# Decay attention and two FFNs: the decay mask is read from rows of powers in SBUF, one load per head on two queues, in place of through HBM

## The chip, the core and the metric

One core of a Trainium2 chip runs the whole program. The metric is device time of one execution in microseconds (us), median of three runs. Five engines work side by side and wait for each other by semaphores: PE (matmul; PEld is its weight load), DVE, ACT and POOL (elementwise), and SP, which here only issues DMA transfers. Sixteen DMA engines carry out the transfers that SP or another engine issues.

## The reference

`q`, `k`, `v` have the shape (2, 8, 768, 64), `lam` one decay per head (8 numbers between 0.97 and 0.99). In blocks of 64 the reference computes causal attention with decay and no softmax, `intra[i, j] = (q_i . k_j) * lam^(i-j)` for `i >= j` and 0 otherwise, plus the share of a running state `kv_state` of 64 x 64 per head, which decays by `lam` per position. The result, as a matrix of 1536 tokens x 512, goes through two FFNs: `(h * tanh(softplus(h))) @ w_out` with `h = x @ w_in` and 2048 hidden columns, then `(g * clip(g + 3, 0, 6) / 6) @ w_out2` in the same sizes. All in fp32.

## The kernel before, in words

The tokens are cut into 12 chunks of 128 (`NCH`), six per batch, and into 3 blocks of 512 (`NBLK`). A chunk is one tile `raw` of 128 x 2048 fp32, loaded in two halves of 512 KB: `load_raw(c, 0)` brings keys and queries with features on partitions, `load_raw(c, 1)` keys and values with positions on partitions. Keys and values come from the host in reversed order of position.

For each chunk, `scores` forms key-query products for 8 heads (two tiles `sc` of 128 x 4 x 128, 16 matmuls). `weigh` multiplies them on DVE by the decay mask into `amat`, and on POOL scales the keys by one column of the same mask (`reverse`, line 170) and the queries by the powers (`lampow`, line 172). `attend` forms the new state `u` (line 191) and the output `o` (lines 197 and 205). `settle` carries the state on and splits `o` into a high and a low part, `X`. Chunks 0 to 3 are done ahead of everything else; the rest are laid between the steps of the FFNs by a written table (`att_at`).

`decay_tables` (lines 116 to 147) makes the mask. It loads `lam` into `small`, writes 127 zeros and a one per head into the HBM tile `z` (line 123), forms 128 powers per head by doubling on DVE (line 129, seven multiplies, into `table`, whose first half is `lampow`), writes them into `z` behind the one (line 135), and reads the mask back with two loads (line 141, 256 KB each). Row `j` of a head's mask is the 128 numbers of that head's row of `z` that start at position `j`, so the 128 rows overlap, each shifted by one number. No partition holds the mask before that.

The FFN weights come as 8-byte numbers. `load_w` stages them and `convert` turns them into fp32 high and low parts, with three passes on ACT and three on DVE per unit (lines 245 to 256, then 67 and 70). `gemm1` (line 272) and `gemm2` (line 285) take three matmul passes per product. They make up 2304 of the matmuls.

All transfers are issued by SP in the order of the code in the prologue (`keep_in_program_order` pins an issue behind what was traced before it on its engine): `lam`, the zeros and the one, `raw` of chunk 0 first half, the first weight unit, the powers, `raw` of chunk 0 second half, the two mask loads, `raw` of chunks 1 to 3, the second weight unit. The rest of the order on each engine is made by a planner that simulates the program. It inserts the semaphore waits too, and the transfers share a small set of semaphores in rotation, so that an issue can wait until an earlier transfer with its semaphore has landed. `warm_up` matmuls on zeros (10, then 16) fill PE while the first data come. ACT's first work after its table load is line 245 on the first weight unit.

Of the kernel before, what the change touches and what calls it, by code (L numbers as in the profile page):

```python
# [7 lines left out]
F32 = mybir.dt.float32  # L8
# [6 lines left out]
ACTF = mybir.ActivationFunctionType  # L15
ALU = mybir.AluOpType
PSUM = bass.MemoryType.PSUM
DRAM = bass.MemoryType.DRAM


@with_exitstack
def decay_attention__mish_ffn__hswish_ffn_kernel(
# [8 lines left out]
    nc = tc.nc  # L31
# [10 lines left out]
    tm2_p = ctx.enter_context(tc.tile_pool(name="tm2", bufs=2, side="right"))  # L42
    tm1_p = ctx.enter_context(tc.tile_pool(name="tm1", bufs=1, side="right"))
    stage_p = ctx.enter_context(tc.tile_pool(name="stage", bufs=2, side="right"))
    dram_p = ctx.enter_context(tc.tile_pool(name="dram", bufs=1, space=DRAM))
    ps_h = ctx.enter_context(tc.tile_pool(name="ps_h", bufs=2, space=PSUM))
    ps_y = ctx.enter_context(tc.tile_pool(name="ps_y", bufs=4, space=PSUM))
    ps_a = ctx.enter_context(tc.tile_pool(name="ps_a", bufs=2, space=PSUM))
# [20 lines left out]
    def split_lo(lo, hi, src):  # L69
        nc.vector.tensor_tensor(out=lo, in0=src, in1=f32(hi), op=ALU.subtract)  # L70

    z = dram_p.tile([8, 256], F32, name="z")
    mask = at1.tile([128, 2, 4, 128], F32, name="mask")
    state = [at1.tile([128, 4, 64], F32, name=f"state{i}") for i in range(2)]
    amat = [at1.tile([128, 4, 128], F32, name=f"amat{i}") for i in range(2)]
# [2 lines left out]
    lampow = table[:, 0].rearrange("p (a i) -> p a i", a=4)  # L78
# [14 lines left out]
    def load_raw(c, i):  # L93
        if c >= NCH:
            return
        if i == 0:
            pool = lent_p if c in (2, 3) else raw_p
            raw_t[c] = pool.tile([128, 2048], F32, tag="raw", name="raw")
        s = slice(i * 1024, (i + 1) * 1024)
        ins = nc.sync.dma_start(out=raw_t[c][:, s], in_=att[c, :, s])  # L100
        if pinned[0]:
            tc.keep_in_program_order(ins)
# [13 lines left out]
    def decay_tables():  # L116
        small = tm1_p.tile([128, 344], F32, tag="th", name="small")
        lam4 = small[:, 0:4].unsqueeze(2)
        head = small[0:8, 8:136]
        tc.keep_in_program_order(nc.sync.dma_start(out=small[:, 0:4], in_=lam))  # L120
        nc.vector.memset(head[:, 0:127], 0.0)
        nc.vector.memset(head[:, 127:128], 1.0)
        tc.keep_in_program_order(nc.sync.dma_start(out=z[:, 0:128], in_=head))
        load_raw(0, 0)
        load_w(*plan[0])
        nc.vector.tensor_copy(lampow[:, :, 0:1], lam4)
        m = 1
        while m < 128:
            nc.vector.tensor_tensor(  # L129
                out=lampow[:, :, m:2 * m], in0=lampow[:, :, 0:m],  # L130
                in1=lampow[:, :, m - 1:m].to_broadcast([128, 4, m]), op=ALU.mult,
            )
            m *= 2
        base = z[0:1, 128:129]
        tc.keep_in_program_order(nc.sync.dma_start(
            out=bass.AP(base.tensor, base.offset, [[256, 2], [512, 4], [1, 128]]), in_=lampow[0:128:64],
        ))
        load_raw(0, 1)
        for h2 in range(2):
            base = z[h2:h2 + 1, 0:1]  # L140
            tc.keep_in_program_order(nc.sync.dma_start(
                out=mask[:, h2],
                in_=bass.AP(base.tensor, base.offset, [[1, 128], [512, 4], [1, 128]]),
            ))
        load_raw(1, 0)
        load_raw(1, 1)

# [83 lines left out]
    def load_w(w, t, half, count):  # L231
        shape = [128, count, 512]
        s = stage_p.tile(shape, U64, tag=f"st{count}", name="st")
        ins = nc.sync.dma_start(out=s, in_=w[t:t + count, half].rearrange("t p n -> p t n"))
        if pinned[0]:
            tc.keep_in_program_order(ins)
        stage_t[t, half] = s
# [163 lines left out]
    nc.scalar.preload_act_table_set("mish")  # L401
    warm_up(10)
    decay_tables()
    load_raw(2, 0)
    load_raw(2, 1)
# [140 lines left out]
```

## Time and profile before

| what | value |
|---|---|
| time, median of 3 runs | 590.46 us (588.24 to 592.97) |
| the profiled execution's own time | 589.52 us |
| its span | 587.5 us |
| PE busy | 577.5 us (98%) |
| DVE, ACT, POOL busy | 270.5, 246.8, 14.8 us |
| bytes through the DMA engines | 50.27 MB |
| mean granted TensorE clock | 1.0 |

The span is the profiled stretch of one execution, the time that of the whole execution; the rows below have their zero at the span's start. Busy shares are means over a prologue (chunks 0 to 3, up to 27.8 us), a stretch in which the FFN steps, the other chunks and the conversion of the weights share the engines, and a long rest of FFN steps alone.

### The profile page before, as it was taken

How to read it: one execution, taken by the hardware profiler on the slowest of the kernel's cores; microseconds unless marked ns; L12 is line 12 of the kernel's file. 1: busy time of each engine (PE TensorE's matmuls, PEld its weight loads, DVE VectorE, ACT ScalarE, POOL GpSimd, SP SyncE). 2: the span in 40 equal slices, each digit the busy share in tenths (PEclk: the TensorE clock that was granted, in tenths of full speed). 3: DMA queues.
4: the chain of work that ended last, by engine and by line, in shares of the span. 5: the costliest groups of instructions: out<-in, count | busy, mean ns of one | idle time of the engine just before them, and what ended most of it. 6: DMA issues, size and time to landing. Idle time of an engine off the chain costs nothing.

```text
span 587.5 us, 7414 instructions
## 1 busy us (share of the span) xinstructions
PE 577.5 (98%) x3034; PEld 470.4 (80%) x3034; DVE 270.5 (46%) x400; ACT 246.8 (42%) x408; POOL 14.8 (3%) x20
## 2 busy tenths in 40 slices
PE   7999999999999999999999999999999999999997
PEld 3877788888888888888888888888888888888885
DVE  4799886423666665511667862222222222222221
ACT  2477764215666665512566652212422222421222
POOL 1600100000000000000000000000000000000000
PEclk9999999999999999999999999999999999999999
DMA  7977754201444333200243220000100000100001
GB/s 222 411 281 254 232 179 144 73 1 73 118 134 143 134 117 108 72 1 0 83 140 137 73 71 0 2 0 1 71 1 0 2 0 1 71 1 0 1 0 71
DMA packets 15546, 50.27 MB, mean 86 GB/s; under 512 B 1674, under 2 KB 2714, under 8 KB 15514
## 3 DMA queue, kind: packets, MB, share of 16 engines
q1 hardware_dynamic: 15514, 49.82, 24.8%
q8 instruction: 23, 0.38, 0.3%
q14 instruction: 9, 0.07, 0.0%
HBM read 46.66 MB, written 3.15 MB: 85 GB/s over the span
## 4 chain that ended last, share of the span: by engine, by line
PE 91%; DMA 4%; DVE 2%; ACT 1%; POOL 0%; issue 0%; SPq 0%; ACTq 0%; POOLq 0%
PE y L285 43%; PE h L272 43%; DMA st<-w 2%; PE sc L154 2%; PE o L205 1%; PE o L197 1%; PE u L191 1%; DMA mask<-z 1%; DVE W L70 1%; ACT st L245 0%; DMA z<-table 0%; DVE st L253 0%; ACT st L246 0%; POOL raw L170 0%; DVE table L129 0%
## 5 line engine op out<-in xcount | busy, mean ns | idle before, releaser
L272 PE MATMUL h<-X,W 128*128 128x512 f32 x1152 | 279.4, 391 | 0.0
L272 PEld LDWEIGHTS h<-X,W 128*128 128x128 f32 x1152 | 214.9, 188 | 46.6 <-issue 1.4
L285 PE MATMUL y<-g,W 128*128 128x512 f32 x576 | 138.8, 389 | 0.9 <-ACT W L67 0.8
L285 PE MATMUL y<-W,g 128*128 128x512 f32 x576 | 138.0, 389 | 0.0
L285 PEld LDWEIGHTS y<-g,W 128*128 128x128 f32 x576 | 107.9, 188 | 23.9 <-ACT W L67 0.9
L285 PEld LDWEIGHTS y<-W,g 128*128 128x128 f32 x576 | 108.1, 188 | 22.4
L70 DVE TENSOR_TENSOR g<-x,g 128x512 fp32r<-128x512 f32 x96 | 66.3, 690 | 74.5 <-ACT g L308 44.8
L318 DVE SCALAR_TENSOR_TENSOR x<-x,h 128x512 f32<-128x512 f32 x48 | 33.0, 688 | 141.5 <-ACT x L311 141.3
L311 ACT ACTIVATE x<-h 128x512 f32<-128x512 f32 x48 | 28.8, 599 | 140.8 <-PE h L272 140.5
L253 DVE SCALAR_TENSOR_TENSOR st<-st 128x512 int32<-128x512 int32 (+1 forms) x57 | 43.1, 757 | 38.9 <-ACT st L246 38.8
L245 ACT ACTIVATE st<-st 128x512 f32<-128x512 f32 (+1 forms) x57 | 41.8, 733 | 43.0 <-DMA st<-w 41.4
L67 ACT ACTIVATE W<-st 128x512 fp32r<-128x512 f32 (+1 forms) x57 | 41.4, 728 | 31.7 <-DVE st L256 31.6
L70 DVE TENSOR_TENSOR W<-st,W 128x512 fp32r<-128x512 f32 (+1 forms) x57 | 43.4, 766 | 23.4 <-ACT W L67 22.5
L307 ACT ACTIVATE x<-h 128x512 f32<-128x512 f32 x48 | 28.5, 595 | 57.4 <-PE h L272 57.4
L67 ACT ACTIVATE g<-x 128x512 fp32r<-128x512 f32 x48 | 30.4, 633 | 32.2 <-DVE x L318 32.0
L256 DVE SCALAR_TENSOR_TENSOR st<-st 128x512 int32<-128x512 int32 (+1 forms) x57 | 43.2, 757 | 1.5
L246 ACT ACTIVATE st<-st 128x512 int32<-128x512 uint16 (+1 forms) x57 | 41.2, 723 | 0.0
L308 ACT ACTIVATE g<-h 128x512 fp32r<-128x512 f32 x48 | 28.4, 592 | 0.0
L179 DVE TENSOR_TENSOR amat<-sc,mask 128x512 f32<-128x512 f32 x24 | 16.1, 686 | 8.0 <-PE sc L154 4.5
L67 ACT ACTIVATE X<-o 128x512 fp32r<-128x512 f32 x12 | 7.1, 590 | 24.2 <-PE o L205 18.7
L154 PEld LDWEIGHTS sc<-raw 64*128 64x128 f32 x192 | 12.6, 187 | 5.1 <-issue 2.6
L154 PE MATMUL sc<-raw 64*128 64x128 f32 x192 | 15.1, 285 | 1.1 <-DVE state L220 1.0
(33 smaller groups left out, 138.0 us busy)
## 6 DMA issues: line engine op xcount, KB each, us to landing
st<-w SPq DMA_DIRECT2D x50, 512.0 KB, 3.3
raw<-att SPq DMA_DIRECT2D x24, 512.0 KB, 4.9
st<-w SPq DMA_DIRECT2D x7, 1024.0 KB, 7.2
out<-o SPq DMA_DIRECT2D x12, 256.0 KB, 2.0
mask<-z SPq DMA_DIRECT2D x2, 256.0 KB, 3.9
small<-lam SPq DMA_DIRECT2D x1, 2.0 KB, 1.6
z<-small SPq DMA_DIRECT2D x1, 4.0 KB
z<-table SPq DMA_DIRECT2D x1, 4.0 KB
```

The costliest lines, as they stand in the source:

```text
L67: nc.scalar.activation(out=hi, in_=src, func=ACTF.Copy)
L70: nc.vector.tensor_tensor(out=lo, in0=src, in1=f32(hi), op=ALU.subtract)
L154: nc.tensor.matmul(sc[h2][:, p, :], lhsT=kT[r, p, :], rhs=qT[r, p, :], start=True, stop=True)
L245: nc.scalar.activation(out=hf, in_=hf, func=ACTF.Copy, scale=2.0 ** -112)
L246: nc.scalar.activation(out=lo16[..., 0] if sign_on_act else lo, in_=lo16[..., 1], func=ACTF.Copy, scale=2.0 ** -13, bias=2.0 ** -14 - 0.5,)
L253: nc.vector.scalar_tensor_tensor(out=lo, in0=hi, scalar=-2 ** 31, in1=lo, op0=ALU.bitwise_and, op1=ALU.bitwise_or)
L256: nc.vector.scalar_tensor_tensor(out=hi, in0=hi, scalar=3, in1=lo, op0=ALU.logical_shift_left, op1=ALU.bitwise_or)
L272: nc.tensor.matmul(h, lhsT=W[t][:, a, kt * 128:kt * 128 + 128], rhs=X[k][:, b, kt, :], start=(kt, a, b) == order[0], stop=(kt, a, b) == or ...
L285: nc.tensor.matmul(y[e], lhsT=l, rhs=r, start=(first and i == 0), stop=(last and i == 2),)
L307: nc.scalar.activation(out=x, in_=h, func=ACTF.Mish)
L311: nc.scalar.activation(out=x, in_=h, func=ACTF.Relu, bias=3.0)
L318: nc.vector.scalar_tensor_tensor(out=r, in0=r, scalar=6.0, in1=h_t.pop(n), op0=ALU.min, op1=ALU.mult)
```

## The change

The HBM tile `z` and the three kinds of transfers through it are gone. `z` becomes an SBUF tile of 128 x 4 x 256 in a slot of the weight staging pool (tag `st2`, two slots): on every partition, for each of four heads, 127 zeros, a one and 128 powers. Partitions 0 to 63 hold the powers of the heads with `h2 = 0`, partitions 64 to 127 those with `h2 = 1`, as `lam` is laid out. The zeros and the one are now written by POOL, the powers are formed directly in `z` by the same DVE instructions, and one more DVE copy brings them to `lampow`. The mask is read with eight transfers of 64 KB, each from one partition (`h2 * 64 + p * 16`), as 128 overlapping rows of 512 B, to 128 partitions. Four are issued on SP (`p` = 0, 2), four on ACT (`p` = 1, 3). `load_raw(0, 1)` stands behind them in the code; before, it stood ahead of the mask loads.

```diff
     def decay_tables():
         small = tm1_p.tile([128, 344], F32, tag="th", name="small")
         lam4 = small[:, 0:4].unsqueeze(2)
-        head = small[0:8, 8:136]
+        z = stage_p.tile([128, 4, 512], F32, tag="st2", name="z")[:, :, 0:256]
+        pw = z[:, :, 128:256]
         tc.keep_in_program_order(nc.sync.dma_start(out=small[:, 0:4], in_=lam))
-        nc.vector.memset(head[:, 0:127], 0.0)
-        nc.vector.memset(head[:, 127:128], 1.0)
-        tc.keep_in_program_order(nc.sync.dma_start(out=z[:, 0:128], in_=head))
+        nc.gpsimd.memset(z[:, :, 0:127], 0.0)
+        nc.gpsimd.memset(z[:, :, 127:128], 1.0)
         load_raw(0, 0)
         load_w(*plan[0])
-        nc.vector.tensor_copy(lampow[:, :, 0:1], lam4)
+        nc.vector.tensor_copy(pw[:, :, 0:1], lam4)
         m = 1
         while m < 128:
             nc.vector.tensor_tensor(
-                out=lampow[:, :, m:2 * m], in0=lampow[:, :, 0:m],
-                in1=lampow[:, :, m - 1:m].to_broadcast([128, 4, m]), op=ALU.mult,
+                out=pw[:, :, m:2 * m], in0=pw[:, :, 0:m],
+                in1=pw[:, :, m - 1:m].to_broadcast([128, 4, m]), op=ALU.mult,
             )
             m *= 2
-        base = z[0:1, 128:129]
-        tc.keep_in_program_order(nc.sync.dma_start(
-            out=bass.AP(base.tensor, base.offset, [[256, 2], [512, 4], [1, 128]]), in_=lampow[0:128:64],
-        ))
+        nc.vector.tensor_copy(lampow, pw)
+        for h2 in range(2):
+            for p in range(4):
+                src = z[h2 * 64 + p * 16:h2 * 64 + p * 16 + 1, p, 0:1]
+                queue = nc.sync if p % 2 == 0 else nc.scalar
+                tc.keep_in_program_order(queue.dma_start(
+                    out=mask[:, h2, p], in_=bass.AP(src.tensor, src.offset, [src.ap[0], [1, 128], [1, 128]]),
+                ))
         load_raw(0, 1)
-        for h2 in range(2):
-            base = z[h2:h2 + 1, 0:1]
-            tc.keep_in_program_order(nc.sync.dma_start(
-                out=mask[:, h2],
-                in_=bass.AP(base.tensor, base.offset, [[1, 128], [512, 4], [1, 128]]),
-            ))
         load_raw(1, 0)
         load_raw(1, 1)
```

## Rows read from the trace of the kernel before

**Rows 1.** Windows: us, busy (count) of PE, PEld, DVE, ACT, POOL; clock, DMA share, GB/s.

```profile
0.00:12.00 12.00, 9.16 (x44) 4.05 (x44) 5.07 (x16) 3.17 (x4) 0.30 (x5) 1.00 0.66 194
12.00:28.00 16.00, 14.49 (x241) 12.10 (x240) 9.91 (x18) 4.68 (x8) 10.78 (x12) 1.00 1.01 401
28.00:60.00 32.00, 31.06 (x231) 24.03 (x232) 30.16 (x38) 24.29 (x33) 0.00 (x0) 1.00 0.78 272
100.00:300.00 200.00, 200.00 (x997) 164.59 (x997) 98.80 (x149) 97.37 (x174) 0.62 (x1) 1.00 0.26 85
```

**Rows 2.** Chain that ended last, prologue: start us, us, what.

```profile
4.47 2.52 DMA z<-table
...
7.50 4.24 DMA mask<-z
...
15.49 1.07 POOL raw L170
```

**Rows 3.** Timeline of SP's issues: start us, us, line, tiles, count.

```profile
0.74 0.38 SPq L120 DMA_DIRECT2D small<-lam  x1
...
1.69 0.36 SPq L100 DMA_DIRECT2D raw<-att  x1
2.09 0.43 SPq L234 DMA_DIRECT2D st<-w  x1
...
5.12 0.40 SPq L100 DMA_DIRECT2D raw<-att  x1
7.07 0.94 SPq L141 DMA_DIRECT2D mask<-z  x2
8.05 3.68 SPq L100 DMA_DIRECT2D raw<-att  x6
```

**Rows 4.** Windows of 1 us: the mask loads, then whole rows of `raw`.

```profile
9.00:10.00 1.00, 1.00 (x6) 0.29 (x4) 0.69 (x1) 0.25 (x1) 0.00 (x0) 1.00 1.00 257
...
16.00:17.00 1.00, 0.40 (x13) 0.40 (x14) 1.00 (x3) 0.54 (x1) 1.00 (x2) 1.00 1.04 426
```

**Rows 5.** Timeline of ACT and DVE up to the second chunk.

```profile
2.39 0.17 DVE L126 COPY table<-small 128x4 f32<-128x4 f32 x1 [1.12 <-DMA small<-lam]
...
7.03 0.66 ACT L245 ACTIVATE st<-st 128x512 f32<-128x512 f32 x1 [5.01 <-DMA st<-w]
8.29 0.69 DVE L253 SCALAR_TENSOR_TENSOR st<-st 128x512 int32<-128x512 int32 x1 [3.85 <-ACT st L246]
...
10.44 0.69 DVE L70 TENSOR_TENSOR W<-st,W 128x512 fp32r<-128x512 f32 x1 [0.73 <-ACT W L67]
11.05 1.47 DVE L179 TENSOR_TENSOR amat<-sc,mask 128x512 f32<-128x512 f32 x2
13.75 0.42 DVE L220 COPY state<-u 128x256 f32<-128x256 f32 x1 [1.23 <-PE u L191]
...
15.75 1.29 DVE L179 TENSOR_TENSOR amat<-sc,mask 128x512 f32<-128x512 f32 x2 [1.57 <-PE o L197]
```

**Rows 6.** Timeline of PE, from the warm-up to the second chunk.

```profile
1.19 4.95 PE L86 MATMUL wp<-wz 128*128 128x512 bf16 x13 [1.19 <-DVE wz L81]
...
7.17 2.98 PE L86 MATMUL wp<-wz 128*128 128x512 bf16 x13
...
11.79 0.43 PE L197 MATMUL o<-amat,raw 128*64 128x128 f32 x2 [1.65 <-DVE amat L179]
...
14.17 0.97 PEld L154 LDWEIGHTS sc<-raw 64*128 64x128 f32 x16 [0.27 <-DMA raw<-att]
...
15.26 0.65 PE L197 MATMUL o<-amat,raw 128*64 128x128 f32 x6
```

**Rows 7.** Timeline of POOL: the table's copy, the second chunk's keys.

```profile
12.90 0.61 POOL L428 COPY table<-mask 128x512 f32<-128x512 f32 x1
...
15.49 1.06 POOL L170 TENSOR_TENSOR raw<-raw,mask 128x512 f32<-128x512 f32 x1 [0.61 <-DMA raw<-att]
```

**Rows 8.** SP's own waits: line, what for, us in total, times, longest.

```profile
SPq L100 <- DMA raw<-att: 6.0, 1, 6.0
```

More of the change, by code (lines that the diff above doesn't have):

```diff
@@ L17 @@
 PSUM = bass.MemoryType.PSUM
-DRAM = bass.MemoryType.DRAM
 @with_exitstack
@@ L44, in decay_attention__mish_ffn__hswish_ffn_kernel @@
     stage_p = ctx.enter_context(tc.tile_pool(name="stage", bufs=2, side="right"))
-    dram_p = ctx.enter_context(tc.tile_pool(name="dram", bufs=1, space=DRAM))
     ps_h = ctx.enter_context(tc.tile_pool(name="ps_h", bufs=2, space=PSUM))
@@ L70, in split_lo @@
         nc.vector.tensor_tensor(out=lo, in0=src, in1=f32(hi), op=ALU.subtract)
-    z = dram_p.tile([8, 256], F32, name="z")
     mask = at1.tile([128, 2, 4, 128], F32, name="mask")
```

## The prediction

> **What bounds the kernel now.** I read the windows by stage first. From 28 us on PE is busy in 31.06 of 32 us, and from 100 to 300 us in all of it [rows 1]: the long rest is matmuls in a fixed number, and nothing in the change touches them. PE can only gain or lose time ahead of that, in the prologue. There, from 0 to 12 us, PE shows 9.16 us busy, but most of it is the two warm-up batches of 4.95 and 2.98 us [rows 6], which are filler. From 12 to 28 us the DMA share is 1.01 at 401 GB/s [rows 1]: the transfers are then at their limit, and in order.
>
> Then I read the chain of waits through the prologue [rows 2]. It runs through the powers' way into HBM (2.52 us from 4.47) and the mask's way back (4.24 us from 7.50). At 15.49 it stands at POOL's scaling of the second chunk's keys, which had idled 0.61 us for its half of `raw` [rows 7]. So two things set the pace: the mask up to 11.74, and behind it the stream of `raw` halves that SP could issue only after the mask loads (5.12, 7.07, 8.05) [rows 3]. Shortly before, PE's scores of chunk 1 wait for `raw` too, and the last six matmuls of chunk 0's output stand behind them in PE's order, done at 15.91 [rows 6]. A shift of that stream by x us shifts the end by nearly x us, since PE is full afterwards.
>
> **The change, part by part.**
>
> *The first transfers.* Without the write of zeros SP issues the first half of `raw` right behind `lam`, at 0.74 + 0.38 = 1.12 in place of 1.69 [rows 3], 0.57 us earlier; the first weight unit likewise. ACT started on that unit at 7.03 [rows 5]; now about 6.5.
>
> *POOL's memsets and DVE's new copy.* 128 x 508 and 128 x 4 zeros and ones on POOL: between nothing and the 0.61 us that its copy of 128 x 512 takes [rows 7]. I take 0.6. POOL has 0.30 us of work up to 12 us [rows 1], and DVE waits for `lam` until 2.39 [rows 5], so this is hidden; without that cover it is 0.6 us. The two small DVE memsets go from the same gap: no gain. The copy into `lampow` lies between 0.42 (128 x 256 copy) and 0.69 us (a 128 x 512 pass with two inputs) [rows 5]; it sits in DVE's idle 3.85 us before 8.29, and the mask loads read `z`, not `lampow`. Cost nothing; uncovered, up to 0.7. The seven multiplies keep their shapes and still end near 4.45.
>
> *The removed trip.* The 2.52 us of writing the powers go entirely [rows 2]. Late next is the mask's own transfer.
>
> *The eight issues.* An issue takes 0.36 to 0.61 us of its queue [rows 3], so four take 1.4 to 2.4 us on each, from 4.47 on. ACT idles 5.01 us before 7.03 [rows 5], and its line 245 now stands behind its four issues: about 6.5, no cost so long as these wait for nothing else. On SP the second half of chunk 0 moves from 5.12 to at least 6.1, and the next six halves from 8.05 to about 6.5 or later. An issue can also wait for an earlier transfer's landing, as one did for 6.0 us [rows 8]; here those are the mask loads and the first unit, behind which the `raw` halves stand anyway. Extra cost zero, included in the next item.
>
> *The transfer itself* is the large unknown: the trace before has no load that reads all its rows out of one partition. The bound below is the mask load before, 512 B pieces from a few KB of HBM, when all sixteen engines together moved 257 GB/s [rows 4]: 524,288 B take 2.0 us. The bound above comes from asking what one partition can give. No row shows one source partition feeding more than one engine's worth of data. An engine moves 426/16 = 26.6 GB/s on long rows and 257/16 = 16.1 GB/s on 512 B pieces [rows 4]. At these rates a 64 KB load takes 2.46 or 4.1 us, and the four that stand one behind another in a queue 9.8 or 16.3 us. I take 9.8: the limit is then one of the memory's side, which the length of a piece does not cut, and the two queues draw from different partitions side by side.
>
> [...]
>
> *The sum.* The mask loads on SP start behind the first unit, at 6.5, and end at 16.3. Behind them on the same queue come three `raw` halves, each 524,288 B at 401 GB/s [rows 1] = 1.3 us: the last lands at 20.2, where 15.49 was the time before [rows 2]. From there the order of work is the one of before, 4.7 us later: 589.52 + 4.7 = **594.2 us**. The base is the profiled execution, 0.94 us under the median shown; I leave it uncorrected. No change, in the sense of 1%, which is about what a measurement of this kernel can tell (5.9 us: below 584.6 or above 596.4).
>
> **Rivals.**
>
> *A. The partition is no bottleneck: 586.8 us, chance 0.33.* The eight loads move like the old ones, 2.0 us behind 6.5, and `raw` lands at 9.8, 11.1 and 12.4, over 3 us earlier. Then DVE is late next: its passes on the first unit end 0.57 us earlier than 11.13, at 10.6, its two mask products (0.69 each) end at 12.0, chunk 0's output about 1.0 later, and the product of chunk 1 starts at 13.0 in place of 15.75 [rows 5]: 2.7 us gained. For it: the old loads read a region as small and were not slow. Against: that was HBM, not one partition.
>
> *B. One partition gives only what an engine draws in 512 B pieces: 600.7 us, slower, chance 0.15.* 16.3 us for the masks; the third half at 6.5 + 16.3 + 3.9 = 26.7, 11.2 us late. Its place is the source partition. It decides "slower" once the shift is over 6.9 us, that is masks over 12.0 us, or a partition under 21.8 GB/s. For it: each row starts 4 B further on, so the pieces are as ragged as the old ones. PE would also idle longer. The granted clock is 1.00 in every window of rows 1, yet the first batch of 13 warm-ups, after 1.19 us of idleness, took 4.95 us and the second 2.98 [rows 6], so a few matmuls after a long wait may be slower; I price this at zero, since the waits for `raw` hide it.
>
> *C. The two queues give no overlap: 604 us, chance 0.07.* The change would then not do what it says. If an engine that stands at one partition's data holds up the other queue's, the eight loads go in series: 8 x 2.46 = 19.7 us, the third half at 30.1, 14.6 late. For it: both queues feed the same sixteen engines, whose share is what the windows count. Against: sixteen engines needn't stand at the same partition together. [...]
>
> **How the numbers follow.** Forecast 0.45, A 0.33, B 0.15, C 0.07. The forecast's own range is 589.5 (four partitions serving at once, 4.9 us in place of 9.8) to 597. All together: 586 to 600 leaves out C, half of B and the lower edge of A, about 0.2. Slower by over 1%: B, C and a tenth of the forecast's case, 0.27. Faster: the edge of A, 0.03. Within 1%: 0.70.
>
> **What would show it.** In the changed kernel: the zeros' and the powers' transfers gone, the first halves issued 0.57 us earlier; the eight issues within about 2 us of 4.47 on SP and ACT; the median time to landing of mask loads growing along each queue by about 2.5 us per load (forecast), 0.5 or less (A), 4 (B), 5 (C); a DMA share near 1 at about 53 GB/s between 7 and 16 us; `raw` of chunk 1 landing near 20 (forecast) or 12 (A); POOL's second scaling there; PE idle up to 18; and from 28 us on the same stages as before, shifted. The prediction is wrong if landings stay close together, if other work of PE fills the wait, or if the planner lays the prologue out in another order.

## The result, and the profile after

The changed kernel took 598.55 us in the median of four runs (596.04 to 605.77) beside 589.9 for the kernel before; the ratio is 1.0108 [1.0074, 1.0143]. (The ratio leaves out disturbed runs on either side, so it is not the quotient of the medians.) So it is slower by some 6.4 us, just past the prediction's 1% bound, which the interval still holds. It lies inside the 586 to 600 that the prediction gives to all its cases together, but above the 589.5 to 597 of the forecast's own case, and 4.3 us above its number. The profiled execution took 598.51 us, span 596.5, which is 9.0 us more than the profiled one before. That one had a mean granted clock of 1.00, and executions of one kernel differ in it: of fifty of the kernel before that were timed beside the experiments, the four at 1.00 took 588.1 to 589.2 us, the three at 0.988 595.2 to 596.6. So the 9.0 are laid against a good execution.

Windows of the changed kernel by stage (columns as in [rows 1]):

```profile
0.00:12.00 12.00, 9.59 (x42) 4.22 (x42) 2.52 (x10) 2.23 (x3) 0.77 (x6) 1.00 0.65 119
12.00:28.00 16.00, 8.81 (x74) 7.10 (x76) 5.71 (x9) 1.51 (x3) 5.29 (x6) 0.57 0.87 273
28.00:60.00 32.00, 31.80 (x334) 25.81 (x333) 29.12 (x40) 22.80 (x32) 6.74 (x7) 1.00 0.83 297
...
100.00:300.00 200.00, 200.00 (x1038) 164.53 (x1034) 97.39 (x147) 96.82 (x173) 1.24 (x2) 1.00 0.27 86
```

Against [rows 1] the loss is all in the prologue. From 12 to 28 us PE ran 74 matmuls instead of 241. The granted clock was 0.57 there, and 1.00 before. From 100 to 300 us PE is busy throughout at a clock of 1.00, as before.

Timeline of SP in the changed kernel (answers to [rows 3]), then of ACT and of POOL (answer to [rows 5, 7]):

```profile
1.20 0.41 SPq L97 DMA_DIRECT2D raw<-att  x1
...
4.55 5.57 SPq L136 DMA_DIRECT2D mask<-z  x4
10.17 8.34 SPq L97 DMA_DIRECT2D raw<-att  x7
```

```profile
4.55 6.45 ACTq L136 DMA_DIRECT2D mask<-z  x4
11.05 0.65 ACT L240 ACTIVATE st<-st 128x512 f32<-128x512 f32 x1 [9.04 <-issue]
```

```profile
16.70 0.61 POOL L423 COPY table<-mask 128x512 f32<-128x512 f32 x1 [15.41 <-DMA mask<-z]
17.64 1.33 POOL L165 TENSOR_TENSOR raw<-raw,mask 128x512 f32<-128x512 f32 x1 [0.33 <-DMA raw<-att]
21.72 1.06 POOL L165 TENSOR_TENSOR raw<-raw,mask 128x512 f32<-128x512 f32 x1 [2.75 <-DMA raw<-att]
```

The last mask load is there at 16.70 (11.74 before, [rows 2]), the second half of chunk 0 at 17.64, that of chunk 1 at 21.72 (15.49 before). Each queue takes 5.6 to 6.5 us for its four issues, and ACT's first conversion stands behind them until 11.05.

PE of the changed kernel, from the end of the warm-up to the first `gemm1` (answers to [rows 6]):

```profile
8.66 2.32 PE L83 MATMUL wp<-wz 128*128 128x512 bf16 x10
17.71 1.98 PE L192 MATMUL o<-amat,raw 128*64 128x128 f32 x16 [6.73 <-DMA raw<-att]
20.39 2.08 PE L149 MATMUL sc<-raw 64*128 64x128 f32 x16 [0.70 <-DMA raw<-att]
23.25 1.29 PE L192 MATMUL o<-amat,raw 128*64 128x128 f32 x6 [0.78 <-DVE amat L174]
24.47 2.07 PE L149 MATMUL sc<-raw 64*128 64x128 f32 x14
26.47 1.02 PE L186 MATMUL u<-raw 128*64 128x64 f32 x16
27.42 0.49 PE L149 MATMUL sc<-raw 64*128 64x128 f32 x2
27.84 0.69 PE L186 MATMUL u<-raw 128*64 128x64 f32 x16
...
38.18 3.01 PE L267 MATMUL h<-X,W 128*128 128x512 f32 x12
```

Two things are to be seen. The order is not that of [rows 6]: `o` of chunk 0 comes first, and its `u`, second before, only at 26.47. And a group of 16 score matmuls takes 2.08 us where it took 1.16 before. The clock in windows of 1 us says why (last three columns: clock, DMA share, GB/s):

```profile
12.00:13.00 1.00, 0.00 (x0) 0.00 (x0) 0.00 (x0) 0.24 (x1) 0.00 (x0) 1.00 0.68 36
13.00:14.00 1.00, 0.00 (x0) 0.00 (x0) 0.67 (x2) 0.00 (x0) 0.00 (x0) 0.80 0.74 86
14.00:15.00 1.00, 0.00 (x0) 0.00 (x0) 0.62 (x2) 0.00 (x0) 0.00 (x0) 0.50 1.10 294
...
26.00:27.00 1.00, 1.00 (x14) 0.78 (x14) 0.00 (x0) 0.00 (x0) 0.00 (x0) 0.50 0.61 250
27.00:28.00 1.00, 1.00 (x18) 0.81 (x16) 0.42 (x1) 0.00 (x0) 0.01 (x1) 0.88 0.28 102
```

PE had nothing to do from 10.98 to 17.71. Within that wait the clock fell to half, 0.50 of full speed, and came back only behind 27 us; 0.80 and 0.88 as means of their windows put the two changes at about 13.6 and 27.2.

The first `gemm1` thus starts 10.4 us later than before (27.80). From there to the end of the span it is 558.3 us, before 559.7: 1.4 us are regained, and 9.0 stay.

### The profile page after: what moved, and what is told of

Read it like the earlier page. It is cut to its first block, busy times and chain, and to the rows that moved or that the text cites. A ratio compares the mean times of both kernels' runs of the same rounds, so it can differ in the third digit from the quotient of the medians.

```text
span 596.5 us, 7428 instructions
## 1 busy us (share of the span) xinstructions
PE 582.0 (98%) x3034; PEld 474.4 (80%) x3034; DVE 270.7 (45%) x399; ACT 246.0 (41%) x408; POOL 16.5 (3%) x22
## 4 chain that ended last, share of the span: by engine, by line
PE 89%; DVE 4%; DMA 3%; ACT 1%; SPq 1%; POOL 1%; issue 1%; ACTq 0%; DVEq 0%; POOLq 0%
PE h L267 42%; PE y L280 42%; PE sc L149 2%; DMA raw<-att 1%; PE o L192 1%; DVE st L248 1%; PE o L200 1%; SPq L136 1%; DMA st<-w 1%; DVE W L68 1%; DVE st L251 1%; PE u L186 1%; ACT st L241 1%; DVE amat L174 1%; SPq L97 0%
## 5 line engine op out<-in xcount | busy, mean ns | idle before, releaser
L192 PE MATMUL o<-amat,raw 128*64 128x128 f32 x192 | 15.1, 293 | 7.7 <-DMA raw<-att 6.7
L149 PEld LDWEIGHTS sc<-raw 64*128 64x128 f32 x192 | 15.0, 215 | 6.6 <-issue 3.1
L149 PE MATMUL sc<-raw 64*128 64x128 f32 x192 | 17.8, 315 | 1.7 <-DMA raw<-att 0.9
```

The lines of the kernel that those rows point to most:

```text
L149: nc.tensor.matmul(sc[h2][:, p, :], lhsT=kT[r, p, :], rhs=qT[r, p, :], start=True, stop=True)
```

## The experiments

Milestones in us from the span's start. "Masks" is the start of POOL's first operation on a complete mask (line 423), "chunk 0" PE's first matmul that uses the mask. All rows but the first have one and the same order of PE's groups between the last two milestones, so that they can be laid side by side.

| kernel | masks | chunk 0 | first `gemm1` | between |
|---|---|---|---|---|
| before (other order) | 11.74 (last load lands) | 11.79 | 27.80 | 16.01 |
| b1_raw_behind | 11.09 | 13.55 | 30.12 | 16.57 |
| x5_hbm | 11.66 | 14.75 | 33.08 | 18.33 |
| x6_half_rows | 11.57 | 12.93 | 33.56 | 20.63 |
| x2_step4 | 13.14 | 16.43 | 34.62 | 18.19 |
| x8_interleaved | 13.34 | 15.76 | 35.83 | 20.07 |
| changed | 16.70 | 17.71 | 38.18 | 20.47 |
| x4_one_queue | 17.01 | 18.81 | 39.81 | 21.00 |
| x1_one_partition | 25.45 | 26.97 | 49.00 | 22.03 |

The times don't follow from these milestones alone. From the first `gemm1` to the end of the span it is 558 to 560 us in the profiles of the kernel before, the changed one, b1_raw_behind, x2_step4, x4_one_queue and x8_interleaved, but 562.4 in x5_hbm, 565.0 in x6_half_rows, 565.6 in x10_first_raw_ahead and 565.8 in x1_one_partition. In these four the granted clock fell a second time: its mean from 60 to 100 us is 0.91, 0.87, 0.91 and 0.87, and 1.00 in the others. As an example x10_first_raw_ahead, where PE was idle for 2.1 of the 10 us in which it fell:

```profile
60.00:70.00 10.00, 7.86 (x53) 5.76 (x53) 8.17 (x12) 7.82 (x11) 1.47 (x1) 0.94 0.76 226
70.00:80.00 10.00, 10.00 (x68) 7.98 (x69) 6.31 (x8) 6.05 (x7) 0.76 (x1) 0.72 0.41 156
```

So the milestones, and not the times, show what an edit does to the prologue.

### The source: one, two or four groups of partitions

x1_one_partition: the four heads of a half all come from one partition.

```diff
-                src = z[h2 * 64 + p * 16:h2 * 64 + p * 16 + 1, p, 0:1]
+                src = z[h2 * 64:h2 * 64 + 1, p, 0:1]
```

> The eight loads read from partitions 0 (h2 = 0) and 64 (h2 = 1) only, so that both queues draw from one partition at a time; the order on every engine is that of the changed kernel. Theory of the source (one partition, or what it shares with its neighbours, hands out some 25 GB/s however many engines ask): the four loads of a half now share one source, 256 KB at 25 GB/s = 10.5 us per half, the masks end near 26 us in place of 16.7, the time goes to about 608 us. Rival, each piece read from SBUF is slow by itself, or eight issues are: nothing changes, masks at 16.7 us, about 598 us.

Measured: masks at 25.45, where 26 was expected, and 616.54 us (a single run) in place of 608. In its profile the clock is at 0.50 from 16 to 36 us, besides the second fall.

x2_step4: partitions 0, 4, 8, 12 (and 64 more) in place of 0, 16, 32, 48.

```diff
-                src = z[h2 * 64 + p * 16:h2 * 64 + p * 16 + 1, p, 0:1]
+                src = z[h2 * 64 + p * 4:h2 * 64 + p * 4 + 1, p, 0:1]
```

> Source partitions h2*64 + 4p in place of h2*64 + 16p, same order on every engine. If the limit is the single partition, nothing changes: masks at 16.7 us, about 598 us. [...] If loads from neighbours close by share more than those 16 apart, it gets slower.

Measured: masks at 13.14, and not near the 16.7 that a limit of the single partition would leave, but a ratio of 1.0158 [1.0104, 1.0213] and a median of 598.34 us (595.88 to 602.26): masks and first `gemm1` come 3.6 us earlier than in the changed kernel, and the time doesn't show it over the spread of the executions. The same two windows of x1_one_partition, of the changed kernel and of x2_step4, a stretch in which nearly only mask loads run:

```profile
7.00:9.00 2.00, 2.00 (x16) 1.05 (x15) 0.00 (x0) 0.00 (x0) 0.00 (x0) 1.00 0.66 25
9.00:11.00 2.00, 2.00 (x10) 0.77 (x8) 0.00 (x0) 0.00 (x0) 0.00 (x0) 1.00 0.65 25
```

```profile
7.00:9.00 2.00, 2.00 (x16) 1.03 (x15) 0.00 (x0) 0.00 (x0) 0.00 (x0) 1.00 0.71 51
9.00:11.00 2.00, 1.98 (x10) 0.69 (x7) 0.00 (x0) 0.00 (x0) 0.00 (x0) 1.00 0.73 73
```

```profile
7.00:9.00 2.00, 2.00 (x16) 1.05 (x15) 0.00 (x0) 0.00 (x0) 0.00 (x0) 1.00 0.70 103
9.00:11.00 2.00, 2.00 (x10) 0.73 (x8) 0.13 (x1) 1.23 (x2) 0.00 (x0) 1.00 0.71 89
```

From 7 to 9 us these are 25, 51 and 103 GB/s (from 9 us on, loads of the second half, with sources of their own, probably run into those of the first). One partition gives 25 GB/s. In the changed kernel the four partitions of a half (0, 16, 32, 48) give only twice that, in x2_step4 (0, 4, 8, 12) four times. So the former make up two sources, and the latter four. Partitions 0 and 16 are probably not the ones that share: the first loads on SP and ACT, which read them, land 4.8 and 5.0 us after their issue in the changed kernel, nearly as soon as the quickest load of x1_one_partition (4.6), while their 131,072 B at 25 GB/s from one source would move for 5.2 us, an estimate. Which partitions do share, no run shows. The DMA share of 0.66, 0.71 and 0.70 at 25, 51 and 103 GB/s says how little that column tells here. It also shows that the limit is not that one engine carries a source, since 0.66 of sixteen engines is more than ten.

x4_one_queue: all eight loads on SP.

```diff
-                queue = nc.sync if p % 2 == 0 else nc.scalar
+                queue = nc.sync
```

> All eight mask loads on SP. Theory of the source: one source at a time, 8 x 2.5 = 20 us from 6.5, masks near 26 us, about 608 us. Rival, the two queues give no overlap: unchanged, 16.7 us, 598 us.

Measured: 600.91 us (a single run), masks at 17.01 instead of 16.70, against 26 expected. A miss: loads that stand in one queue are carried out side by side, and one queue draws as fast as two. Its eight issues took 7.52 us together, each load landed 4.4 to 6.5 us after its issue, and from 7 to 9 us 50 GB/s moved, beside 51 in the changed kernel:

```profile
7.00:9.00 2.00, 2.00 (x12) 0.94 (x11) 0.64 (x1) 1.22 (x2) 0.00 (x0) 1.00 0.70 50
9.00:11.00 2.00, 1.61 (x8) 0.52 (x6) 0.74 (x2) 0.67 (x1) 0.00 (x0) 1.00 0.69 59
```

x6_half_rows: only the second half of each mask row is loaded, 256 B in place of 512, and POOL writes zeros into the first 64 columns; those of the mask are left out.

```diff
-        nc.vector.tensor_copy(lampow, pw)
+        nc.vector.tensor_copy(lampow, pw); nc.gpsimd.memset(mask[:, :, :, 0:64], 0.0)
...
-                src = z[h2 * 64 + p * 16:h2 * 64 + p * 16 + 1, p, 0:1]
+                src = z[h2 * 64 + p * 16:h2 * 64 + p * 16 + 1, p, 64:65]
...
-                    out=mask[:, h2, p], in_=bass.AP(src.tensor, src.offset, [src.ap[0], [1, 128], [1, 128]]),
+                    out=mask[:, h2, p, 64:128], in_=bass.AP(src.tensor, src.offset, [src.ap[0], [1, 128], [1, 64]]),
```

> Each of the eight loads brings only the second half of every row (256 B in place of 512 B, 128 pieces each); the first 64 columns of the mask are set to zero, so part of the decay product is left out. If the source gives so many bytes a second, the masks need half the time and end near 11.5 us in place of 16.7. If it gives so many pieces a second, they still end near 16.7.

Measured: masks at 11.57, 59 GB/s from 7 to 9 us; 600.34 us (a single run). Half the bytes in as many pieces take 7.0 us from the first issue at 4.56, where the changed kernel takes 12.15. So the limit is one of bytes, not of pieces, which takes away rival B's rate of 16.1 GB/s. As an estimate from the two: 262,144 B less save 5.14 us, so the whole 524,288 B take 10.3 us and begin to move at 6.4.

### Without the slow source

x5_hbm: the powers' rows go once to HBM, and the eight loads read from there, on both queues as in the changed kernel.

```diff
-        nc.vector.tensor_copy(lampow, pw)
+        nc.vector.tensor_copy(lampow, pw); zd = dram_p.tile([8, 256], F32, name="zd"); base = zd[0:1, 0:1]; tc.keep_in_program_order(nc.sync.dma_start(out=bass.AP(base.tensor, base.offset, [[256, 2], [512, 4], [1, 256]]), in_=z[0:128:64]))
...
-                src = z[h2 * 64 + p * 16:h2 * 64 + p * 16 + 1, p, 0:1]
+                src = zd[2 * p + h2:2 * p + h2 + 1, 0:1]
...
-                    out=mask[:, h2, p], in_=bass.AP(src.tensor, src.offset, [src.ap[0], [1, 128], [1, 128]]),
+                    out=mask[:, h2, p], in_=bass.AP(src.tensor, src.offset, [[1, 128], [1, 128]]),
```

> The changed kernel with its eight loads on two queues and raw behind them, but the rows (zeros, one, powers) are written once to HBM from two partitions and read from there. Theory of the source: pieces from HBM take 27 ns and not some 230, the eight loads end by about 11 us, and the time is near the kernel before, 589 to 592 us. Rival, the structure of the change is at fault (eight issues, two queues, raw behind the mask, the planner's new order): the time stays at 596 to 599 us.

Measured: masks at 11.66, as in the kernel before, and yet a ratio of 1.0098 [1.0062, 1.0134]. The slow source is not the whole loss. Chunk 0 starts at 14.75, since its second `raw` half stands behind the mask loads on SP, and the clock falls here too, for a shorter time, to a mean of 0.80 from 13 to 16 us and 0.72 from 16 to 20: PE's first two groups take 1.97 and 1.89 us. The first `gemm1` is 5.1 us earlier than in the changed kernel, but 4.1 of them are lost again behind it in the profiled execution, with the second fall of the clock; so the time, which can't be told from the changed kernel's 1.0108, is no measure of what the source costs.

b1_raw_behind: the kernel before, with nothing but `load_raw(0, 1)` moved to its place in the changed one.

```diff
-        load_raw(0, 1)
         for h2 in range(2):
...
             ))
+        load_raw(0, 1)
         load_raw(1, 0)
```

> The kernel before, mask through HBM and all on SP, with one line moved: the second half of raw of chunk 0 is issued behind the two mask loads, as in the changed kernel. The planner answers with the changed kernel's order on PE (chunk 0's output first, its state update u only after most of the scores of chunk 2). Theory that part of the loss is this move and the order it brings, whatever the source of the mask: the masks land as before (11.7 us), that half of raw at 12.5 to 14.5 us, chunk 0 starts there, and the first gemm1 runs at 30.5 to 33 us in place of 27.80, the time is 592 to 595 us (3 to 5 us slower). Rival, the move costs only the landing (0.7 us) and the rest of the loss needs the SBUF source or the eight issues: first gemm1 near 28.5 us, 590 to 591 us.

Measured: 1.0043 [1.0014, 1.0072], 2.5 us where 3 to 5 were expected. PE of b1_raw_behind:

```profile
13.55 1.09 PE L197 MATMUL o<-amat,raw 128*64 128x128 f32 x16 [3.46 <-DMA raw<-att]
14.76 1.16 PE L154 MATMUL sc<-raw 64*128 64x128 f32 x16
16.70 0.43 PE L197 MATMUL o<-amat,raw 128*64 128x128 f32 x2 [0.78 <-DVE amat L179]
17.30 0.44 PE L197 MATMUL o<-amat,raw 128*64 128x128 f32 x4 [0.17 <-DVE amat L179]
17.66 1.16 PE L154 MATMUL sc<-raw 64*128 64x128 f32 x14
18.75 0.69 PE L191 MATMUL u<-raw 128*64 128x64 f32 x16
19.36 0.49 PE L154 MATMUL sc<-raw 64*128 64x128 f32 x2
19.78 0.69 PE L191 MATMUL u<-raw 128*64 128x64 f32 x16
...
22.07 1.16 PE L154 MATMUL sc<-raw 64*128 64x128 f32 x16
...
30.12 3.06 PE L272 MATMUL h<-X,W 128*128 128x512 f32 x12
```

Moving that one load is enough for the planner's other order (`o` first, `u` late), at the full clock throughout. It is the ruler for the changed kernel: group for group, the changed kernel stands 4.16 us later at the first `o`, 5.63 at the first scores, 6.55 at the next `o`, 6.81, 7.72, and 8.06 from the second `u` on, up to the first `gemm1`. The shift grows only while the clock is at half, and stops growing when it is back.

### The clock

x3_warm: 46 warm-up matmuls in place of 16 before the scores of chunk 1, so that PE is busy until the masks land.

```diff
-    warm_up(16)
+    warm_up(46)
```

> 46 in place of 16 warm-up matmuls on zeros ahead of the scores of chunk 1, which fill PE's idle time from 10.98 to 17.71 us (30 more at 0.23 us = 6.8 us); the planner also lays chunk 0's state update earlier. Theory that 4 us of the loss come from the granted clock of 0.50 between 14 and 27.6 us: the clock stays at 1.00, the matmuls of 17.7 to 28 us take 4.7 instead of 8.9 us, and the time falls by 2.5 to 4.5 us, to 594 to 596 us. Rival, the prologue is bound by the arrival of raw and PE's pace doesn't matter: no gain (within 1 us of 598).

Measured: 601.08 us, 1.0178 [1.0139, 1.0218]: a miss. PE was busy up to 17.5 and the clock at 1.00 up to 20, but the planner laid the groups in another order (scores of chunk 1 first, at 19.75), with 2.27, 2.36 and 2.28 us of waits in it, and the clock fell twice later (means of 0.64 from 20 to 24 and 0.84 from 32 to 36). It changes two things and decides nothing.

p1_pinned, p2_pinned_warm: to hold the order fixed, every compute instruction from the second warm-up on is pinned to the order of the code, and p2_pinned_warm has 56 warm-ups in place of 16 besides.

```diff
-    nc = tc.nc
+    class Pinned:
...
+            return lambda *a, **k: tc.keep_in_program_order(op(*a, **k)) if held[0] else op(*a, **k)
...
+    nc = Core()
...
-    warm_up(16)
+    held[0] = True
+    warm_up(56)
```

> The changed kernel with every compute instruction from the second warm-up on pinned to the order of the code on its engine, so that p2 can be compared with it. PE then waits from the end of the warm-up (11 us) for raw of chunk 1 (20 us). By itself it only sets the base: the whole program in the order of the code may cost some us or tens of us, 600 to 640 us.

> p1_pinned with 56 in place of 16 warm-up matmuls in the second batch; the order on PE, DVE, ACT and POOL is that of p1 otherwise. Theory, the granted clock of 0.50 after PE's long wait costs time of its own: the clock stays at 1.00 up to the first gemm1, chunk 0 to 2 run at the full pace, and the first gemm1 and the time come 2 to 4 us earlier than in p1. Rival, the slow matmuls hide behind the arrival of raw and behind DVE: less than 1 us.

Measured: 677.34 and 676.24 us (1.1471 [1.1427, 1.1516] and 1.1458 [1.1406, 1.151]), over the 600 to 640 expected of p1_pinned, since the pinned order costs far more than what is studied here; the first `gemm1` at 37.60 and 36.69. From 12 to 20 us and from 20 to 28 us the clock was 0.58 and 0.78 in p1_pinned and 1.00 in p2_pinned_warm, and that gave 0.9 us, where 2 to 4 were expected. The theory as it stood then fell. PE of p2_pinned_warm shows where the rest of it went:

```profile
19.87 1.16 PE L36 MATMUL sc<-raw 64*128 64x128 f32 x16 [0.32 <-DMA raw<-att]
...
23.23 1.16 PE L36 MATMUL sc<-raw 64*128 64x128 f32 x16 [0.71 <-DMA raw<-att]
...
35.60 1.16 PE L36 MATMUL sc<-raw 64*128 64x128 f32 x14 [2.12 <-DVE state L36]
```

In this order the second scores at 23.23 wait for `raw`, and the scores at 35.60 for DVE (2.11 us in p1_pinned as well). The slow groups of p1_pinned fill the first of these waits (24.05 there, without a wait).

In the planner's own order the price is larger, and can be read without a new kernel. x4_one_queue and b1_raw_behind have the same order, the same wait of 0.78 us for DVE, and no wait for `raw` between chunk 0's start and `gemm1`. PE of x4_one_queue:

```profile
18.81 1.98 PE L192 MATMUL o<-amat,raw 128*64 128x128 f32 x16 [8.20 <-DMA raw<-att]
20.71 2.08 PE L149 MATMUL sc<-raw 64*128 64x128 f32 x16
23.57 1.29 PE L192 MATMUL o<-amat,raw 128*64 128x128 f32 x6 [0.78 <-DVE amat L174]
...
28.57 1.12 PE L186 MATMUL u<-raw 128*64 128x64 f32 x16
29.48 1.49 PE L192 MATMUL o<-amat,raw 128*64 128x128 f32 x10
30.90 1.51 PE L200 MATMUL o<-raw,state 64*64 64x128 f32 x16
32.34 1.16 PE L149 MATMUL sc<-raw 64*128 64x128 f32 x16
...
39.81 3.02 PE L267 MATMUL h<-X,W 128*128 128x512 f32 x12
```

The stretch takes 21.00 us here and 16.57 there. Up to the scores at 32.34, which stand at 22.07 in b1_raw_behind, the groups that ran at half the clock cost 5.0 us; 0.6 come back behind them, where b1_raw_behind waits for DVE. That comparison came after the runs, and no edit changes the clock alone in this order. Executions of one kernel do differ in it: of b1_raw_behind's, the three at a mean clock of 1.00 took 590.2 to 591.6 us, the four at 0.988 595.0 to 598.0. So a lower clock goes with a longer time in one and the same program; where it fell in these is not recorded.

### Can the change be saved

x8_interleaved: x2_step4 with the loop over heads outside, so that each queue alternates between the halves, eight sources in all.

```diff
-        for h2 in range(2):
-            for p in range(4):
-                src = z[h2 * 64 + p * 16:h2 * 64 + p * 16 + 1, p, 0:1]
+        for p in range(4):
+            for h2 in range(2):
+                src = z[h2 * 64 + p * 4:h2 * 64 + p * 4 + 1, p, 0:1]
```

> Source partitions h2*64 + 4p as in x2_step4, and the loads alternate between the two halves, so that all eight sources are in use at once; the order on PE, POOL and SP is that of the changed kernel. So far the masks ended at 25.4 us with one source per half, 16.7 with the changed kernel's, 13.1 with four per half. Theory, each such group of sources gives about 25 GB/s and engines that are ahead draw from the next: 8 x 25 = 200 GB/s, 512 KB in 2.6 us, masks near 10 us, raw behind them, first gemm1 at 31 to 32 us, 591 to 594 us. Rival, four sources are already enough and the rest of the wait is the issue of the loads: masks stay near 13 us, 595 us or more.

Measured: 111 GB/s from 7 to 9 us against 103, masks at 13.34, ratio 1.0138 [1.0084, 1.0193]: eight sources in turn give hardly more than four. What holds them back is not shown: 25 GB/s from each of the eight would make 200, an estimate, and the issues on each queue took from 4.54 to 9.05, so that the issuing may be the limit here.

x9_raw_ahead: x8_interleaved with all masks on ACT, and `raw` of chunk 0 and 1 ahead of them on SP.

```diff
+        load_raw(0, 1)
+        load_raw(1, 0)
+        load_raw(1, 1)
...
-                queue = nc.sync if p % 2 == 0 else nc.scalar
+                queue = nc.scalar
...
-        load_raw(0, 1)
-        load_raw(1, 0)
-        load_raw(1, 1)
```

> x8_interleaved with the mask loads all on ACT, and the halves of raw for chunks 0 and 1 issued on SP right behind the first weight unit. Theory, what is left of the loss in x8 is raw that stands behind the masks: here raw of chunk 1 is there by 11 us, the masks by 11 us as well, the first gemm1 runs at 25 to 27 us (27.80 in the kernel before), and the time is 586 to 589 us, 1 to 3 under the kernel before. Rival, the masks now share the DMA engines with raw and ACT is held up by eight issues until about 10 us: no gain on the kernel before (589 to 593 us).

Measured: 1.010 [1.0066, 1.0134], a miss. DVE in x9_raw_ahead:

```profile
17.80 0.69 DVE L174 TENSOR_TENSOR amat<-sc,mask 128x512 f32<-128x512 f32 x1 [3.59 <-DMA mask<-z]
```

`raw` moved at 402 GB/s from 7 to 9 us, and the masks, issued from 4.62 on, were first usable at 17.80; in x8_interleaved, from the same sources, all were there at about 13.3. Two things differ, the `raw` beside the masks and one queue for all eight issues (7.63 us on ACT, against 4.5 on each of two queues), and no run separates them.

x10_first_raw_ahead: x8_interleaved with only `load_raw(0, 1)` ahead of the masks, as in the kernel before.

```diff
+        load_raw(0, 1)
         nc.vector.tensor_copy(pw[:, :, 0:1], lam4)
...
-        load_raw(0, 1)
         load_raw(1, 0)
```

> x8_interleaved with one thing more: the second half of raw of chunk 0 is issued on SP ahead of the mask loads, as in the kernel before; four mask loads on SP, four on ACT. [...] Theory: the masks end by 10.5 to 11.5 us, chunk 0's output starts within 2 us of the end of the warm-up at 10.5, so the clock stays at 1.00, the first gemm1 runs at 27 to 29 us and the time is that of the kernel before (588 to 591 us). Rival, the loss sits elsewhere in the changed structure (ACT held by its issues, another order of the planner): 594 us or more, as x8 and x9.

Measured: 594.88 us, 1.0067 [1.0036, 1.0098], the best of the new kernels, but where its rival had it, 594 or more. Chunk 0 starts at 14.85 and `gemm1` at 31.74, 3.9 us late; the clock is 0.64 from 12 to 20 us and falls again from about 69 on. The profiled execution was the slowest of its ten, 599.34. No version beat the kernel before.

## Why the prediction was right and wrong

**The source's limit: right.** Masks at 16.3 were forecast, 16.7 measured, and chunk 0's half at 17.6, measured 17.64. The two terms behind it hold too, a start at 6.5 and 9.8 us, by the estimate from x6_half_rows (6.4 and 10.3). The rate per source, 26.6 GB/s from one engine's share [rows 4], is near the 25 measured. The picture behind it was wrong in one point: it has the four loads of a queue go one behind another. Loads of one queue run side by side too (x4_one_queue), and what counts is the number of different source groups. There happened to be two of those, as there were two queues, so that the number came out by luck. The sign to look for, landings that grow by 2.5 us per load, came out blurred: from its issue a load took 4.8 to 8.5 us, since the later issues were themselves held.

**Rivals.** A fell: 25 GB/s per partition is a bottleneck, and x2_step4 with twice the rate of the changed kernel brought the masks to 13.1. B fell as a mechanism (x6_half_rows), though its 600.7 us is closer to the time than the forecast's 594.2, by luck. C's words held, a second queue adds no rate (x4_one_queue: masks at 17.01 against 16.70, 50 GB/s from 7 to 9 us against 51). Its price didn't hold: 19.7 us assumed one source at a time.

**Three `raw` halves at 1.3 us each: under-sized.** Chunk 1's second half was forecast for 20.2 and came at 21.72. The transfers moved 205 GB/s from 13 to 16 us, with the last masks, and 261 from 16 to 20, not the 401 of [rows 1]. SP's issues of `raw` took until 18.5. That is 1.5 us.

**"From there the order of work is the one of before": this step failed.** The planner's order changes as soon as `load_raw(0, 1)` stands behind the masks, and b1_raw_behind, with the old mask path, pays 2.3 us for it at the first `gemm1` (30.12 against 27.80). The prediction itself counts another order among the signs of being wrong.

**The clock at a price of zero: this failed too.** The prediction saw in [rows 6] that matmuls ran slower after idleness, 4.95 us instead of 2.98, and argued that "the waits for `raw` hide it". Only the first group's slowness was hidden so. Of the 3.90 us by which the changed kernel's stretch is longer than b1_raw_behind's (20.47 against 16.57), some 0.6 is the wait for `raw` at 20.39 (0.70, less a gap of 0.1 there), and the remaining 3.3 lie in groups at half the clock: 0.9 each in `o` and the two score groups, 0.6 in the others. The 0.9 of the first `o` cost nothing by themselves: the scores behind it waited for `raw` up to 20.39 in any case.

So the first `gemm1` is late by 2.3 (order and place of the load) + 4.2 (chunk 0 later in that order, 17.71 against 13.55) + 1.5 (`raw`, with the first `o` inside its wait) + 2.4 (the other groups at half clock) = 10.4 us, where the forecast had 4.7. This is an account of two traces laid side by side, and at the full clock another wait might have taken some of the 2.4. The 4.2 holds the source limit and the held issues together: x5_hbm, with a fast source, has 1.2 of it (14.75). 1.4 us come back later.

**Small steps.** The first `raw` half was issued 0.49 us earlier, not 0.57. POOL's memsets and DVE's copy were hidden, as forecast. ACT's conversion, forecast for 6.5, began at 11.05: the four issues took 6.45 us and not 1.4 to 2.4. With the masks on SP alone (x4_one_queue) it began at 7.11, and nothing was gained, since PE waited for `raw` in any case. "Extra cost zero" for held issues was thus right on ACT. On SP the issues of `raw` were held until 18.5; what that cost apart from the slow source no run separates.

**Open:** why the first `raw` halves behind the masks move slowly, what part of the 2.5 us of b1_raw_behind is the order and what the later load, and what the slow source costs in time, since no kernel without it (x2_step4, x5_hbm, x8_interleaved) was faster than the changed one clear of noise.

## What to carry to other kernels

Before small loads are read out of SBUF, count the different source groups that they draw from at once, in bytes per second, not the queues that issue them (from one group to four each gave 25 GB/s; eight gave 111 together). Then follow what stands behind them on the queue, and whether moving one load lets the planner lay out another order. A wait on PE may not be paid once: read the granted clock of the stretch behind it, and where it fell, price the groups there at what they take at that clock (16 score matmuls 2.08 us at 0.50, 1.16 at 1.00), unless they wait for something else too. And before a time is put down to an edit, look at the mean granted clock of the executions compared.

## What the runs showed of the hardware that was not expected

One wait of PE, 6.73 us in the changed kernel, left it at half the clock for some 13.6 us, 9.5 of them after the work had come. The length of the last wait alone doesn't tell: in b1_raw_behind one of 3.46 us left the clock at 1.00, while in x3_warm, behind one of 2.27, its mean from 20 to 24 us was 0.64.

An issue is held when loads before it are slow: four issues of mask loads on SP took 1.76 us with the rows in HBM (x5_hbm), 4.11 from four sources (x2_step4), 5.57 from two and 9.31 from one (x1_one_partition). The chain of waits of the changed kernel shows SP's four issues of the masks grow, with the third and the fourth as here:

```profile
5.79 1.59 SPq L136
...
7.42 2.70 SPq L136
```

On ACT the same hold stops its compute work: line 240 starts at 7.17 in x5_hbm, at 11.05 in the changed kernel and at 15.49 in x1_one_partition.

A queue of its own did not keep the mask loads clear of the stream of `raw`: in x9_raw_ahead they took from 4.62 to 17.80 and more, in x8_interleaved, on both queues and with the same sources, they were done at 13.3. How much of that is the stream and how much the single queue is not shown.
